# Expert weights read in 4 KB runs, with the second expert's two products run back to back

## The chip, the cores and the metric

The kernel runs on one core of one Trainium2 chip. The metric is the device time of one execution in microseconds, the median of three runs: 222.31 us before the change (221.52 to 224.03). The profile is of one execution, whose span is 219.5 us by the profiler's clock.

## The reference

Two blocks follow each other. The first is a gated recurrence over four sequences of 5056 steps, 256 channels wide. The second takes each of the 20224 results as a token, picks one of eight experts for it by a gate, keeps per expert the 80 tokens with the largest gate probability, and runs a two-layer network on those. All other rows of the output are zero.

```python
for t in range(S):                       # S = 5056, D = 256, four sequences
    h = f[:, t] * h + (1.0 - f[:, t]) * x[:, t]
    y[:, t] = h
...
logits = x @ w_gate                      # x = y.reshape(20224, 256), 8 experts
expert_idx = np.argmax(logits, axis=1)
gate_w = probs[np.arange(N), expert_idx]
out = np.zeros((N, D), dtype=np.float32)
for e in range(E):                       # the best 80 tokens of each expert
    h = np.maximum(x[tok_idx] @ w1[e], 0.0)            # w1[e]: 256 x 1024
    out[tok_idx] = gate_w[tok_idx, None] * (h @ w2[e])  # w2[e]: 1024 x 256
```

Everything is float32. The inputs of the recurrence are 20.7 MB each, the output is as large, and the experts' weights are 16.8 MB (1 MB for each of the two matrices of an expert).

## The kernel before

**The recurrence.** The sequences are cut into 40 units of 512 steps. For each unit the kernel loads gate and input (`load`, L224 and L227), forms the gate on ScalarE, multiplies on GpSimd, turns both to channels on partitions with TensorE (L247), and scans along time on VectorE (L264), into `h_all`, which stays in SBUF. The gate's logits (L276) and the candidates per expert follow in the same loop, one group of four units behind.

**Clearing the output.** The whole output has to be zero before rows are scattered into it. `clear` copies zeros in pieces of up to 1 MB, all issued from the SP queue: from a spare part of `h_all` while the units run (`clear_some`), from rows of the output that are zero already (DRAM to DRAM, the form with no `zero` given, L158), and from a zero tile in SBUF (L163). `clear_blocks(m)` issues m such blocks. With the last unit's load two blocks go out (L437). Nineteen blocks and a rest are cleared by hand-placed calls. The last one, of 0.75 MB, is issued by the first `more` in the experts' stage.

**Selecting.** After the last unit, VectorE, ScalarE and TensorE work out which 80 tokens each expert keeps (L561 to L645), ending in `trow`, the token numbers by expert. TensorE runs dummy products (`busy`, L181) through these waits.

**The experts.** The order of instructions on each engine is the order in which the code names them; nothing is rearranged. For an expert, `gather` copies its 80 columns out of `h_all` one by one, 24 on VectorE, 32 on ScalarE and 24 on GpSimd (L689); `scaled` multiplies them by a per-channel factor (L698); `hidden` is the first product, 32 products into two tiles `h_ps` (L711); `relu` runs on ScalarE (L720); `result` is the second product, eight products into `y_ps` (L727); `finish` scales the rows on VectorE (L733); `scatter` writes them to their places in the output with an indirect DMA from GpSimd (L736), which has to wait for the clears and for the scatter before it. `settle` (L647) works out where the rows go (`slots_down`: `gsl`, `goal`) and whether the selection was certain (`doubts`). The loop at L767 does, for expert e, the gather of e + 2, the first product of e + 1, the second of e, and the scatter of e - 1.

**The weights.** `weights` (L497) loads a matrix as two halves of 0.5 MB into `wring`, a ring of seven buffers. One of these first holds the zero tile. The halves of the first matrix (`which == 1`, L503) are its two halves of columns: a partition gets two runs of 2 KB. The halves of the second (L507) are its two halves of rows: a partition gets four runs of 1 KB. `order` lists the matrices in the order of loading: first and second of expert 0, first of expert 1, and then in turns the first of e + 1 and the second of e. Three matrices are loaded ahead; `more(1)` issues the next one, whose DMA waits until the buffer that it takes is free. A load and the clears stand in one queue, so a load lands behind all that was issued before it.

In `hidden` a weight load takes 64 neighbouring columns of one half:

```python
halves[i][:, o, ds(c * P + j, P // 2)]   # i: half of the columns, o: half of the input channels
```

Of the kernel before, what the change touches and what calls it, by code (L numbers as in the profile page):

```python
# [23 lines left out]
def kernel(  # L24
# [146 lines left out]
    def clear_blocks(m, zero=None):  # L171
        clear_some(len(zeros) % R, zero)
        for k, _ in zeros[:m * R:R]:
            clear(k, None, zero)
        del zeros[:m * R]
# [7 lines left out]
    with tc.tile_pool(name="ld", bufs=4) as ld, \  # L183
# [237 lines left out]
        for n in range(-AHEAD, n_unit):  # L421
            unit(load, n + AHEAD)
            unit(gate, n + 2)

            g, b = divmod(n - 1, B)
            if g > 0 and b == 0:
                aside(g - 1)
            unit(enter, n + 2)
            unit(lambda m: to_channels(m, sts, sps, pss, "sp"), n + 1)
            unit(lambda m: to_channels(m, uts, ups, psu, "up"), n + 1)  # L430
            unit(decay, n + 1)
            unit(scan, n)
            some_of(of_group, 1)
            for jobs in of_batches:
                some_of(jobs, 1)
            unit(logits, n - 1)
            if n + AHEAD == n_unit - 1:  # L437
                clear_blocks(2)
            elif 2 <= n < n_unit - AHEAD:
                clear_some(1, spare(4 if n < 27 else 2 if n < 31 else 1))  # L440
            if n > 0 and n % B == 0:
                g = n // B - 1
                of_group += [[lambda g=g: by_token(g)]]
                if g < ALONE:
                    of_group[-1] += [lambda g=g: shifted(g)]
                    of_group += [[lambda g=g: chosen(g)]]
# [41 lines left out]
                                        imm_value=-2.0)  # L488


    wring = ctx.enter_context(tc.tile_pool(name="wring", bufs=7))
    FH, CH = F // 2, FC // 2
    order = [(1, 0), (2, 0), (1, 1)]
    for e in range(1, E):
        order += ([(1, e + 1)] if e + 1 < E else []) + [(2, e)]

    def weights(which, e):  # L497
        halves = []
        for i in range(2):
            t = wring.tile([P, DC * FH], F32, name="w_sb", tag="w_sb")  # L500
            if which == 1:
                t = t.rearrange("p (o f) -> p o f", o=DC)
                nc.sync.dma_start(out=t, in_=w1[e][:, ds(i * FH, FH)].rearrange(  # L503
                    "(o p) f -> p o f", p=P))
            else:
                t = t.rearrange("p (c d) -> p c d", c=CH)
                nc.sync.dma_start(out=t, in_=w2[e][ds(i * FH, FH)].rearrange(  # L507
                    "(c p) d -> p c d", p=P))
            halves.append(t)
        return halves  # L510

# [3 lines left out]
    zero = wring.tile([P, R * D], F32, name="w_sb", tag="w_sb")  # L515
    nc.sync.dma_start(out=zero.rearrange("p (k d) -> p k d", k=R), in_=out_z[:, 0:R])
    w_sb[order[0]] = weights(*order[0])
    clear_blocks(5, zero)
    for key in order[1:3]:
        w_sb[key] = weights(*key)  # L520
    clear_blocks(3)
# [21 lines left out]
    def slots_down(flat, sp):  # L543

        nc.tensor.transpose(sp, flat, ident[:2 * E, :2 * E])
        nc.vector.tensor_copy(gsl, sp[:, ds(E, E)])
        far = consts.tile([K, E], F32, name="far", tag="far")
        nc.vector.tensor_scalar(out=far, in0=gsl, scalar1=0.0, scalar2=AWAY,
                                op0=ALU.is_le, op1=ALU.mult)
        nc.vector.tensor_tensor(goal, sp[:, :E], far, ALU.add)  # L550
# [96 lines left out]
    def settle():  # L647


        low = consts.tile([P, DEEP], F32, name="low")  # L650
        d = doubts
        slots_down(flat, kept[:K, ds(K, 2 * E)])
        nc.vector.tensor_scalar(out=low, in0=taken, scalar1=-2.0, scalar2=2.0,  # L653
                                op0=ALU.mult, op1=ALU.add)
        nc.vector.tensor_tensor(low, low, vals, ALU.add)
        nc.vector.tensor_reduce(d[:, 4:5], low, AX.X, ALU.min)
        nc.vector.tensor_reduce(d[:, 5:6], tops[:, :, TOP - 1], AX.X, ALU.max)
        nc.vector.tensor_copy(d[:, 0:1], taken[:, DEEP - 1:])
        nc.vector.tensor_tensor(d[:, 1:2], d[:, 5:6], d[:, 4:5], ALU.is_ge)
        nc.vector.scalar_tensor_tensor(out=d[:, 2:3], in0=vals[:, ds(TOP - 1, 1)],  # L660
                                       scalar=vals[:, ds(TOP, 1)], in1=taken[:, ds(TOP, 1)],
                                       op0=ALU.is_le, op1=ALU.mult)
        nc.vector.tensor_scalar(d[:, 3:4], off[:, 2:3], float(capacity), off[:, 1:2],
                                ALU.min, ALU.not_equal)
# [6 lines left out]
    def experts(again):  # L671
        with tc.tile_pool(name="xp", bufs=2) as xp, \
# [8 lines left out]
            def gather(e, between={}):  # L681
                X[e] = xp.tile([P, DC, K], F32, name="xe", tag="xe")
                k = 0
                for engine, copy, n in ways:
                    _, at_tok = nc.values_load_multi_w_load_instructions(
                        trow[ds(e, 1), ds(k, n)], engines=(engine,), min_val=0, max_val=N - 1,
                        skip_runtime_bounds_check_because="token numbers come from iota")
                    for j, v in enumerate(at_tok):
                        copy(X[e][:, :, ds(k + j, 1)], h_all[:, :, ds(v, 1)])  # L689
                        if copy == nc.scalar.copy and j + 1 in between:  # L690
                            between[j + 1]()
                    k += n
# [7 lines left out]
            def hidden(e):  # L700
                HID[e] = mp.tile([P, FC, K], F32, name="hid", tag="hid")
                xt = XT.pop(e)
                halves = w.pop((1, e))
                ps = []
                for i in range(2):
                    h_ps = psh.tile([P, CH, K], F32, name="h_ps", tag="h_ps")

                    for c in range(CH):
                        for o in range(DC):
                            for j in range(0, P, P // 2):  # L710
                                nc.tensor.matmul(h_ps[ds(j, P // 2), c],  # L711
                                                 halves[i][:, o, ds(c * P + j, P // 2)],
                                                 xt[:, o], start=o == 0, stop=o == DC - 1,
                                                 skip_group_check=True)
                    ps.append(h_ps)
                return ps
# [5 lines left out]
            def result(e):  # L722
                y_ps = psy.tile([K, D], F32, name="y_ps", tag="y_ps")
                halves = w.pop((2, e))
                hid = HID.pop(e)
                for c in range(FC):
                    nc.tensor.matmul(y_ps, hid[:, c], halves[c // CH][:, c % CH],  # L727
                                     start=c == 0, stop=c == FC - 1)
                return y_ps
# [10 lines left out]
            def more(m):  # L740
                for key in late[:m]:
                    w[key] = weights(*key)
                del late[:m]
                clear_blocks(len(clears))
# [9 lines left out]
            gather(1, {8: lambda: relu(0, ps, [0]), 24: lambda: relu(0, ps, [1])})  # L754
            scaled(1)
            more(1)
            gather(2)
            y_ps = result(0)
            more(1)
            scaled(2)  # L760
            if not again:
                settle()
            finish(0, y_ps)
            ps = hidden(1)
            relu(1, ps)
            more(1)
            for e in range(1, E):  # L767
                if e + 2 < E:
                    gather(e + 2)
                if e + 1 < E:  # L770
                    ps = hidden(e + 1)
                    relu(e + 1, ps)
                    more(1)
                y_ps = result(e)
                if e == 1 and not again:
                    total = psl.tile([1, 4], F32, name="total", tag="rivals")
                    nc.tensor.matmul(total, ones, doubts[:, :4], start=True, stop=True)
                more(1)
                if e + 2 < E:
                    scaled(e + 2)  # L780
                finish(e, y_ps)
                scatter(e - 1)
                if e == 1 and not again:
                    found = consts.tile([1, 1], F32, name="found")
                    nc.vector.tensor_reduce(found, total, AX.X, ALU.add)
                    nc.vector.tensor_copy(doubt, found)
                if e == E - 2 and not again:
                    unsure.append(nc.values_load(
                        doubt, min_val=0, max_val=4 * P,
                        skip_runtime_bounds_check_because="a sum of 4 * P flags"))  # L790
# [89 lines left out]
```

## Time and profile before

| What | Value |
|---|---|
| Time, median of three runs | 222.31 us (221.52 to 224.03) |
| Span of the profile | 219.5 us |
| TensorE busy | 195.6 us (89%) |
| VectorE busy | 160.8 us (73%) |
| ScalarE busy | 140.3 us (64%) |
| GpSimd busy | 133.1 us (61%) |
| Bytes moved by DMA | 80.62 MB, 367 GB/s over the span |
| Share of the 16 DMA engines taken by the SP queue | 94.9% |
| Of that, expert weights | 32 loads of 512 KB, 7.1 us from issue to landing (median) |

The page gives each engine's busy time, the chain of work that ended last, and groups of instructions by line, engine and tile. In a line of a group or of the timeline, the name of a tile before the arrow is what is written, the names after it are what is read. PE is a product on TensorE, PEld its weight load, DVE is VectorE, ACT ScalarE, POOL GpSimd, SP the queue that issues the loads and clears. A float32 product appears as two records. Times in a timeline are us from the start of the span. The share of DMA can go slightly over 1, as packets overlap.

### The profile page before, as it was taken

What the parts mean: (1) busy time and instruction counts of PE and PEld (TensorE: products, weight loads), DVE (VectorE), ACT (ScalarE), POOL (GpSimd) and SP (SyncE); (2) the same over time, 40 slices, a digit from 0 to 9 for tenths busy, and PEclk for the clock granted to TensorE, in tenths of its full rate; (3) what the DMA queues carried; (4) which work ended last, traced back from release to release, by engine and by line L of the source; (5) the groups of instructions that cost most, each with busy time, mean ns of one, the idle gap of its engine ahead of it and who ended that gap; (6) DMA issues with size and microseconds to landing.
All of it is one profiled execution on the core that took longest, in us unless ns stands there. A gap on an engine that the chain in (4) does not pass through costs nothing.

```text
span 219.5 us, 6776 instructions
## 1 busy us (share of the span) xinstructions
PE 195.6 (89%) x2145; PEld 151.5 (69%) x2145; DVE 160.8 (73%) x437; ACT 140.3 (64%) x440; POOL 133.1 (61%) x271
## 2 busy tenths in 40 slices
PE   7589999999999699999969999788796789999990
PEld 7457777777777477767747776777775667787750
DVE  5687789797979879899786998995556726665110
ACT  3587786877689967787796875151566754665100
POOL 4489578777876689777649881121557365656021
PEclk9999999999999999999999999999999699999996
DMA  6999999999999999999999998999999999999710
GB/s 154 412 418 417 419 418 420 418 415 419 414 419 417 420 414 419 415 417 417 414 401 296 339 367 275 404 416 388 397 382 332 353 393 394 393 385 375 271 37 21
DMA packets 31564, 80.62 MB, mean 367 GB/s; under 512 B 3232, under 2 KB 12832, under 8 KB 30816
## 3 DMA queue, kind: packets, MB, share of 16 engines
q1 hardware_dynamic: 30592, 79.44, 94.9%
q0 software_dynamic: 384, 0.66, 0.9%
q8 instruction: 19, 0.31, 0.5%
q14 instruction: 25, 0.20, 0.2%
q10 hardware_dynamic: 544, 0.01, 0.1%
HBM read 65.28 MB, written 21.36 MB: 395 GB/s over the span
## 4 chain that ended last, share of the span: by engine, by line
PE 43%; DMA 29%; DVE 9%; issue 7%; POOL 4%; ACT 3%; SPq 2%; POOLq 1%; DVEq 0%; ACTq 0%
DMA out_dram<-y,goal 14%; PE lg L276 12%; PE sp L247 12%; PE up L247 12%; DMA out_dram<-out_dram 11%; DMA x_t<-in_x_dram 4%; POOL x_t L240 4%; PE warm L181 2%; DVE h_all L264 2%; PE lt L292 2%; DVE at L596 1%; ACT f_t L232 1%; PE kept L641 1%; DVE beat L615 1%; SPq L227 1%
## 5 line engine op out<-in xcount | busy, mean ns | idle before, releaser
L240 POOL TENSOR_TENSOR x_t<-f_t,x_t 128x1024 f32<-128x1024 f32 (+2 forms) x40 | 93.4, 2338 | 33.9 <-DMA x_t<-in_x_dram 13.7
L264 DVE TENSOR_TENSOR_SCAN h_all<-h_all,up 128x512 f32<-128x512 f32 (+1 forms) x80 | 95.5, 1243 | 4.7 <-ACT h_all L258 2.7
L258 ACT ACTIVATE h_all<-sp,nomlb 128x512 f32<-128x512 f32 (+1 forms) x80 | 50.0, 677 | 7.3 <-PE sp L247 7.3
L232 ACT ACTIVATE f_t<-f_t 128x1024 f32<-128x1024 f32 (+1 forms) x40 | 42.3, 1059 | 15.7 <-DMA f_t<-in_f_logit_dram 15.7
L247 PEld LDWEIGHTS sp<-ident,f_t 128*128 128x128 f32 (+1 forms) x320 | 34.0, 140 | 19.7 <-issue 10.3
L247 PE MATMUL sp<-ident,f_t 128*128 128x128 f32 (+1 forms) x320 | 43.8, 279 | 2.7 <-ACT h_all L258 2.3
L247 PE MATMUL up<-ident,x_t 128*128 128x128 f32 (+1 forms) x320 | 42.0, 273 | 4.6 <-POOL x_t L240 2.2
L276 PE MATMUL lg<-h_all,wg 128*32 128x128 f32 (+1 forms) x640 | 43.1, 400 | 0.0
L247 PEld LDWEIGHTS up<-ident,x_t 128*128 128x128 f32 (+1 forms) x320 | 35.3, 140 | 6.7 <-POOL x_t L240 3.3
L689 ACT COPY xe<-h_all 128x2 f32 x256 | 25.4, 190 | 14.7 <-issue 11.6
L689 POOL COPY xe<-h_all 128x2 f32 x192 | 24.3, 196 | 13.0 <-issue 11.3
L689 DVE COPY xe<-h_all 128x2 f32 x192 | 22.7, 177 | 12.6 <-issue 12.6
L727 PE MATMUL y_ps<-w_sb,hid 128*80 128x256 f32 x128 | 29.3, 383 | 1.8 <-DMA w_sb<-in_moe_w_dram 1.6
L276 PEld LDWEIGHTS lg<-h_all,wg 128*32 128x32 f32 x640 | 18.4, 118 | 11.7 <-issue 4.3
L727 PEld LDWEIGHTS y_ps<-w_sb,hid 128*80 128x80 f32 x128 | 18.5, 150 | 10.3 <-issue 1.8
L711 PE MATMUL h_ps<-xt,w_sb 128*64 128x80 f32 x512 | 21.0, 244 | 3.9 <-DVE low L653 2.5
L711 PEld LDWEIGHTS h_ps<-xt,w_sb 128*64 128x64 f32 x512 | 19.7, 145 | 5.8 <-issue 3.1
L736 POOL DMA_INDIRECT out_dram<-y,goal x8 | 7.5, 939 | 21.1 <-DMA out_dram<-y,goal 11.3
L181 PE MATMUL warm<-ident 128*128 128x128 f32 x140 | 18.3, 291 | 1.4 <-POOL ident masks.py:199 1.4
L181 PEld LDWEIGHTS warm<-ident 128*128 128x128 f32 x140 | 17.6, 206 | 1.5 <-POOL ident masks.py:199 1.4
L733 DVE TENSOR_SCALAR y<-y_ps,gsl 80x256 f32<-80x256 f32 x8 | 3.8, 478 | 14.1 <-PE y_ps L727 14.1
L720 ACT ACTIVATE hid<-h_ps 128x320 f32<-128x320 f32 x16 | 6.7, 431 | 7.6 <-PE h_ps L711 7.4
(116 smaller groups left out, 100.4 us busy)
## 6 DMA issues: line engine op xcount, KB each, us to landing
f_t<-in_f_logit_dram SPq DMA_DIRECT2D x36, 512.0 KB, 7.9
x_t<-in_x_dram SPq DMA_DIRECT2D x36, 512.0 KB, 8.3
w_sb<-in_moe_w_dram SPq DMA_DIRECT2D x32, 512.0 KB, 7.1
out_dram<-h_all SPq DMA_DIRECT2D x34, 256.0 KB, 8.1
out_dram<-out_dram SPq DMA_DIRECT2D x5, 1024.0 KB, 11.1
out_dram<-w_sb SPq DMA_DIRECT2D x5, 1024.0 KB, 9.7
f_t<-in_f_logit_dram SPq DMA_DIRECT2D x4, 448.0 KB, 6.8
x_t<-in_x_dram SPq DMA_DIRECT2D x4, 448.0 KB, 7.2
```

Source lines behind the costliest of these rows:

```text
L181: nc.tensor.matmul(warm, ident, ident, start=True, stop=True)
L232: nc.scalar.activation(s_t, s_t, ACT.Sigmoid, scale=-1.0)
L240: nc.gpsimd.tensor_tensor(u_t[:, cut:], sts[n][:, cut:], u_t[:, cut:], ALU.mult)
L247: nc.tensor.transpose(ps[:, r:R * k:R], src[n][:, r, ds(o * P, P)], ident[:k, :k])
L258: nc.scalar.activation(columns(n, o), sps.pop((n, o)), ACT.Identity, scale=nomlb[:, ds(o, 1)], bias=1.0)
L264: nc.vector.tensor_tensor_scan(h, h, ups.pop((n, o)), h_all[:, o, ds(spot(n) - 1, 1)] if n >= B else 0.0, ALU.mult, ALU.add)
L276: nc.tensor.matmul(lgs[g][ds(r * LC, LC), b, :k], wg[:, o], columns(n, o)[:, r::R], start=o == 0, stop=o == DC - 1, skip_group_check=True)
L689: copy(X[e][:, :, ds(k + j, 1)], h_all[:, :, ds(v, 1)])
L711: nc.tensor.matmul(h_ps[ds(j, P // 2), c], halves[i][:, o, ds(c * P + j, P // 2)], xt[:, o], start=o == 0, stop=o == DC - 1, skip_group_ch ...
L720: nc.scalar.activation(HID[e][:, ds(i * CH, CH)], ps[i], ACT.Relu)
L727: nc.tensor.matmul(y_ps, hid[:, c], halves[c // CH][:, c % CH], start=c == 0, stop=c == FC - 1)
L736: nc.gpsimd.indirect_dma_start(out=out, out_offset=bass.IndirectOffsetOnAxis(ap=goal[:, ds(e, 1)], axis=0), in_=Y.pop(e), in_offset=None, ...
```

## The change

The change gives every partition one run of 4 KB in each half of the weights. For the first matrix a half is now half of its rows (input channels) with all 1024 columns; for the second, partition p takes the four neighbouring rows 4p to 4p + 3 of a half. The inner channels then have to be counted alike on both sides: channel 4k + c of a half is column k of the c-th product, so a weight load of `hidden` takes 64 columns with a step of four elements, and both halves are needed for each output.

With it goes a new order. The second matrix of expert 1 is loaded ahead of the first of expert 2, and the second product of expert 1 precedes the first of expert 2. `slots_down` is taken out of `settle` and stands before the first product of expert 1, `settle` moves behind the second `finish`, the ReLU of expert 1 moves into ScalarE's gather of expert 2 (after 12 and 24 copies), and the loop starts at expert 2. One block of clears moves from the zero tile (five blocks to four) to the place of the last unit's load (two to three). The aim is longer runs for the DMA engines, fewer waits of TensorE for weights, and work for the DMA queue before the zero tile arrives.

```diff
             if n + AHEAD == n_unit - 1:
-                clear_blocks(2)
+                clear_blocks(3)
...
-    order = [(1, 0), (2, 0), (1, 1)]
-    for e in range(1, E):
+    order = [(1, 0), (2, 0), (1, 1), (2, 1), (1, 2)]
+    for e in range(2, E):
...
             if which == 1:
-                t = t.rearrange("p (o f) -> p o f", o=DC)
-                nc.sync.dma_start(out=t, in_=w1[e][:, ds(i * FH, FH)].rearrange(
-                    "(o p) f -> p o f", p=P))
+                nc.sync.dma_start(out=t, in_=w1[e][ds(i * P, P)])
+                t = t.rearrange("p (i k c) -> p i c k", i=2, c=CH)
             else:
                 t = t.rearrange("p (c d) -> p c d", c=CH)
                 nc.sync.dma_start(out=t, in_=w2[e][ds(i * FH, FH)].rearrange(
-                    "(c p) d -> p c d", p=P))
+                    "(p c) d -> p c d", c=CH))
...
-    clear_blocks(5, zero)
+    clear_blocks(4, zero)
...
-        slots_down(flat, kept[:K, ds(K, 2 * E)])
...
-                                                 halves[i][:, o, ds(c * P + j, P // 2)],
+                                                 halves[o][:, i, c, ds(j, P // 2)],
...
             more(1)
-            gather(2)
             y_ps = result(0)
+            if not again:
+                slots_down(flat, kept[:K, ds(K, 2 * E)])
+            ps2 = hidden(1)
+            gather(2, {12: lambda: relu(1, ps2, [0]), 24: lambda: relu(1, ps2, [1])})
             more(1)
             scaled(2)
+            finish(0, y_ps)
+            y_ps = result(1)
+            more(1)
+            gather(3)
+            ps = hidden(2)
+            relu(2, ps)
+            more(1)
+            scaled(3)
+            finish(1, y_ps)
+            scatter(0)
             if not again:
                 settle()
-            finish(0, y_ps)
-            ps = hidden(1)
-            relu(1, ps)
-            more(1)
-            for e in range(1, E):
+            for e in range(2, E):
```

## The prediction

> **What bounds the kernel now.** I read the page's chain first (the work that ended last), then the stretches table, the timeline of TensorE, the same chain in order of time, and the groups of weight loads.
>
> The page's chain, by engine:
>
> ```profile
> PE 43%; DMA 29%; DVE 9%; issue 7%; POOL 4%; ACT 3%; SPq 2%; POOLq 1%; DVEq 0%; ACTq 0%
> ```
>
> Up to 122 us the chain is TensorE's recurrence work, which the change does not touch; from 134 to 159 us it is VectorE's selection, also untouched. What can move is the stage after 159 us, the experts. TensorE there (h_ps is an expert's first product, y_ps its second; start, length, what the idle time waited for):
>
> ```profile
> 159.46 2.44 PE L711 MATMUL h_ps<-xt,w_sb 128*64 128x80 f32 x64 [1.41 <-issue]
> 162.09 3.78 PE L727 MATMUL y_ps<-w_sb,hid 128*80 128x256 f32 x16 [0.20 <-ACT hid L720]
> ...
> 165.94 2.44 PE L711 MATMUL h_ps<-xt,w_sb 128*64 128x80 f32 x64
> 170.91 3.92 PE L711 MATMUL h_ps<-xt,w_sb 128*64 128x80 f32 x64 [2.54 <-DVE low L653]
> 176.46 3.65 PE L727 MATMUL y_ps<-w_sb,hid 128*80 128x256 f32 x16 [1.62 <-DMA w_sb<-in_moe_w_dram]
> ...
> 180.16 2.43 PE L711 MATMUL h_ps<-xt,w_sb 128*64 128x80 f32 x64
> 182.53 3.68 PE L727 MATMUL y_ps<-w_sb,hid 128*80 128x256 f32 x16
> ```
>
> Call these h0, y0, h1, h2, y1, h3, y2 by expert. From 176.46 us on TensorE has no gap until y7 ends at 213.56: one expert each 5.97 us. Before that lie three losses: 2.5 us idle ahead of h2, 1.5 us in h2 itself (3.92 for 2.43), 1.6 us ahead of y1, which waits for its weights. The DMA queue is why. Stretches (PE, PEld, DVE, ACT and POOL busy, granted clock, DMA share, GB/s):
>
> ```profile
> 134.00:138.00 4.00, 3.29 (x55) 2.06 (x54) 3.55 (x8) 2.63 (x5) 0.00 (x0) 1.00 0.80 227
> 142.00:151.00 9.00, 7.16 (x59) 6.65 (x57) 8.10 (x32) 4.10 (x16) 2.26 (x9) 1.00 1.03 419
> 154.00:155.80 1.80, 1.80 (x19) 1.80 (x18) 0.31 (x3) 0.00 (x0) 0.15 (x2) 1.00 1.08 378
> 162.50:166.00 3.50, 3.50 (x19) 2.06 (x18) 1.67 (x14) 2.11 (x20) 2.04 (x17) 1.00 1.01 321
> 177.00:189.00 12.00, 12.00 (x164) 9.20 (x163) 5.07 (x36) 7.84 (x68) 8.04 (x50) 1.00 1.07 395
> ```
>
> The queue is full (share about 1) except in 134 to 138, and its speed follows the runs: 419 GB/s for the clears in 4 KB pieces (142 to 151), 378 for the second matrix in 1 KB pieces (154 to 155.8), 408 for the first in 2 KB pieces (a stretch at 139), 321 for the clears from DRAM to DRAM (162.5 to 166). In 177 to 189 both TensorE and the queue are full; TensorE wins narrowly, since the slack between a half's landing and its use, read from the landings, grows from 1 us at y2 to 2.5 us at y7. The chain by time shows a second path as long:
>
> ```profile
> 161.23 13.83 DMA out_dram<-out_dram
> ...
> 177.32 5.37 DMA out_dram<-y,goal
> ...
> 211.22 2.30 DMA out_dram<-y,goal
> ...
> 214.35 0.91 POOL out_dram L736
> ```
>
> The last clear, issued at 161.23, lands at 175.06; only then may the first scatter go, and every scatter waits for the one before (5.1 to 5.6 us each while the queue is full, plus 0.8). It ends level with TensorE. So a gain needs both: weights of experts 1 and 2, and the last clear, landing earlier.
>
> **What the Trainium skill says.** *DMA: Bandwidth & Descriptors*, "Why small descriptors are slow (HBM only)": every packet carries a fixed overhead, so short ones run below the engine's rate; the trace agrees (378 against 419 GB/s). *SBUF — State Buffer*, "Door 1: The DMA port swizzle": memory lines are 16 bytes, and an access that crosses to a new line each time pays a penalty. The new weight read steps four fp32, exactly 16 bytes, so every element is on a new line. *TensorE: Matmul & The Clock Gate*, "LDWEIGHTS": a load costs its columns over 1.2 GHz, an estimated 53 ns for 64. The trace agrees: 137 ns for 64 columns, 192 for 128 in a stream, 0.86 ns a column. Same page, "The HAM clock gate": after a mostly idle window of 3.4 us the clock is halved; the trace has one such stretch, 171.6 to 175.0, after the idle time before h2.
>
> **The change part by part.**
>
> *4 KB runs.* A half of 0.524 MB at 378, 408 and 419 GB/s takes 1.39, 1.29 and 1.25 us: 0.14 us saved per half of the second matrix, 0.04 of the first. Up to and with the weights of experts 0 and 1 and the first of expert 2 that is 4 × 0.14 + 6 × 0.04 = 0.8 us. Later, 0.36 us an expert, hidden: TensorE is the bound there. It does shorten the backlog behind which each scatter lands.
>
> *One clear earlier.* A third block clear goes out ahead of the zero tile's load, which waits for buffers until 134.3 us; one clear from the zero tile goes. The bytes stay the same, but the thin stretch 134 to 138 gets work: 4 us × (419 − 227)/419 = 1.8 us of queue at most. The zero tile's load itself is slow there and the four clears after it still wait for its landing, so I take 0.4 to 1.2, and 0.5 with the first part's overlap: the last weights needed for h2 (second half of expert 2) land where y1's second half lands now, 177.64, less 0.8 and 0.5, so about 176.4.
>
> *Order.* Expert 1's second matrix comes ahead of expert 2's first. It takes over the latter's landings, 170.78 and 172.08, less 1.0 to 1.2: about 169.7 and 170.9. h1 ends at 168.4, so y1 runs 169.8 to 173.5 (its second half needs its weights 1.8 us after the start, 171.6). The ReLU that y1 needs now stands inside ScalarE's gather, after 12 and 24 of 32 copies; that gather starts at 166.25 with 98 ns a copy, so the ReLUs come at 167.5 and 169.1, behind no wait that binds. What queues behind them on ScalarE is the rest of the gather, 0.9 us later, for an h2 that waits until 176.4 anyway. Then h2 stands from 176.5 to 178.9. Before, the same four products (h1, h2, y1 after y0) were done at 180.11: 1.2 us gained. The swap alone gives nothing: both weights were needed before h3, and one of the two stages always waits for the last half. The idle time only moves, to 2.9 us between y1 and h2.
>
> *Settling later, slots earlier.* Eleven small VectorE operations of 0.15 to 0.2 us move behind the second finish. The 2.54 us that h2 waited for them vanish, but the weights bind in their place: nothing. The three for the slots go ahead of a gather that has 5 us to spare.
>
> *Halves by input rows.* h needs both halves at its start (one was enough) and frees both at its end: 1.2 us earlier, 1.2 later. With slack of 1 to 2.5 us and a queue that now gains 0.36 us an expert on TensorE, nothing from h3 on; for h2 it is in the 176.4.
>
> *The step of 16 bytes.* The disputed cost: no weight load of h_ps kind has a step in this trace. The nearest rows:
>
> ```profile
> L247 PEld LDWEIGHTS sp<-ident,f_t 128*128 128x128 f32 (+1 forms) x320 | 34.0, 140 | 19.7 <-issue 10.3 <-ACT h_all L258 4.6 <-ACT f_t L232 3.9
> L711 PEld LDWEIGHTS h_ps<-xt,w_sb 128*64 128x64 f32 x512 | 19.7, 145 | 5.8 <-issue 3.1 <-DVE far L548 2.7
> L292 PEld LDWEIGHTS lt<-ident,ls 128*128 128x128 f32 (+1 forms) x40 | 5.5, 207 | 1.6 <-ACT ls L283 1.1
> ```
>
> L247 and L292 are both loads for transposes of 128 columns; L292 reads with the same step of four, and takes 67 ns more, 0.5 ns a column. In a stream, though, its transposes follow each other at 119 ns instead of 109, 0.93 ns a column. h_ps has 32 pairs of loads in 2.43 us, 76 ns a pair. Low end: 0.93 ns a column is a ceiling on the read; 64 columns take 60 ns, still under 76: nothing. Middle: 0.5 ns a column on top of 0.86: 87 ns, 0.4 us a stage. High end: the rate halves as it did for the transposes: 110 ns, 3.7 us a stage. I take nothing, because a plain load already reads at 0.86 ns a column, where the stepped read stands at 0.93.
>
> Sum: 222.3 − 1.2 (TensorE's path; the scatters start about 1.2 us earlier too, at 176.1, and catch up as the backlog shrinks) = 221.1, and 0.1 back for a chance of the cold clock: 221.2.
>
> **Rivals.**
> 1. *More of the queue's loss comes back.* For: 227 GB/s in 134 to 138 is an open 1.8 us, and the DRAM clears run at 423 GB/s at 159 to 161.5 but 321 later. All 1.8 and 0.8 recovered puts h2's weights at 175.0 and its end at 177.5, 2.6 us gained; the freed queue and the scatters' spacing (0.2 us over TensorE's) bring some 0.5: 219.2. Against: the zero tile's load is a chain of its own.
> 2. *The stepped read doubles the weight load.* TensorE is the bound from h2 on, with six h stages left: 6 × 1.25 = 7.5 us, less 1.2: 228.6. h0 and h1 would hide in the wait for weights. For: 207 against 140 ns, and the skill's 16-byte line. Against: the stream's 0.93. With the middle cost 6 × 0.4 − 1.2 = +1.2: 223.5.
> 3. *The idle 2.9 us before h2 halves the clock* for a 3.4 us window (as after 2.54 us before) and the last weights are no earlier: h2 takes 3.9, up to 180.4, and no gain remains, 222.5, or 225 with h4 late as well, whose second half can only be issued when h2 has freed its buffer.
>
> **How the numbers follow.** Forecast 221.2: 0.36, with rival 3's mild form in it (within 1%, 220.1 to 224.5). Rival 1, 219.2: 0.33 (faster by over 1%). Rival 2, 228.6: 0.26, and rival 3's 225: 0.05 (slower, 0.31). The range leaves out the best twentieth and the upper half of rival 2: 218.8 to 228.5.
>
> **What would show it.** Right: weights at about 418 GB/s in a stretch after 177; no thin stretch at 134 to 138; y1 starting at about 169.8, h2 at 176.5 with a wait for its weights; first scatter at 176; h_ps loads of 140 to 150 ns and stages of 2.4 us. Wrong: h_ps stages of 2.8 us or more (rival 2); a wait before h2 under 1 us (rival 1); clock 0.5 after 176 (rival 3). A y1 that waits for its ReLU and not for weights would break the order's step.

## The result, and the profile after

The changed kernel takes 230.89 us (230.38 to 231.33, four runs) where the kernel before, on the same chip, took 223.17 (221.52 to 224.72; the three runs given above and a fourth): a ratio of 1.0346, 95% interval 1.0258 to 1.0435. It is slower by 7.7 us. The forecast was 221.2 us; the nearest case was the second rival, at 228.6.

The page's chain, by engine, of the kernel after:

```profile
PE 63%; DMA 15%; issue 6%; DVE 6%; POOL 4%; ACT 3%; SPq 1%; POOLq 0%; DVEq 0%; ACTq 0%
```

TensorE carries 63% of the chain where it had 43%, and the DMA half of what it had. The clears, and all scatters but the last ones, which together were a second path as long, have left it. The timeline of TensorE says why (start, length, what the idle time waited for; L712 is the first product, L728 the second):

```profile
160.42 4.43 PE L712 MATMUL h_ps<-xt,w_sb 128*64 128x80 f32 x64 [2.27 <-issue]
164.77 3.80 PE L728 MATMUL y_ps<-w_sb,hid 128*80 128x256 f32 x16
...
168.64 4.07 PE L712 MATMUL h_ps<-xt,w_sb 128*64 128x80 f32 x64
172.64 3.68 PE L728 MATMUL y_ps<-w_sb,hid 128*80 128x256 f32 x16
176.76 0.47 PE L712 MATMUL h_ps<-xt,w_sb 128*64 128x80 f32 x4 [0.44 <-DMA w_sb<-in_moe_w_dram]
177.97 7.67 PE L712 MATMUL h_ps<-xt,w_sb 128*64 128x80 f32 x124 [0.74 <-DMA w_sb<-in_moe_w_dram]
185.57 3.68 PE L728 MATMUL y_ps<-w_sb,hid 128*80 128x256 f32 x16
...
189.30 4.07 PE L712 MATMUL h_ps<-xt,w_sb 128*64 128x80 f32 x64
```

From h1 on every first product takes 4.07 us in place of 2.43 (h0 takes 4.43, most of it at a granted clock of 0.50, in 161.64 to 165.05 us); the second product is unchanged at 3.68. The new order did what it was to do: y1 follows h1 without a wait, and in place of the losses ahead of h2 and y1 (2.54 and 1.62 us) stand 0.44 and 0.74 us in h2. But from h2 on nothing hides TensorE, and six stages at 1.64 us more are 9.8 us. The last second product ends at 223.26 us, not 213.56. Where the 1.64 us are, the group of weight loads says (count | busy us, mean ns of one):

```profile
L712 PEld LDWEIGHTS h_ps<-xt,w_sb 128*64 128x64 f32 x512 | 31.7, 217 | 5.3 <-issue 4.4 <-PE y_ps L728 0.8
```

The same load of 64 columns took 145 ns in the mean before (137 at full clock). The stretches show what this does to the queue, and what became of the thin stretch:

```profile
134.00:138.00 4.00, 3.29 (x55) 2.06 (x54) 3.48 (x8) 2.73 (x5) 0.00 (x0) 1.00 1.01 344
138.00:142.00 4.00, 3.19 (x29) 2.95 (x28) 3.60 (x16) 0.65 (x2) 0.98 (x3) 1.00 0.98 346
...
177.00:189.00 12.00, 11.26 (x144) 9.94 (x142) 6.95 (x54) 6.72 (x58) 7.77 (x48) 1.00 0.97 376
189.00:201.00 12.00, 12.00 (x149) 10.33 (x148) 6.70 (x50) 7.56 (x67) 6.90 (x43) 1.00 0.81 284
```

Two of these stretches in the kernel before:

```profile
138.00:142.00 4.00, 3.19 (x29) 2.95 (x29) 3.60 (x15) 0.65 (x2) 0.98 (x3) 1.00 1.04 410
...
189.00:201.00 12.00, 12.00 (x162) 9.23 (x161) 7.86 (x59) 7.95 (x69) 7.90 (x50) 1.00 1.07 386
```

In 134 to 138 us the queue is now full (share 1.01 for 0.80), but at 344 GB/s, and 138 to 142 has dropped to 346, from 410 before. From 189 us on the share is 0.81, where it was 1.07: the queue waits for TensorE to free buffers. TensorE alone is the bound there.

### The profile page after: what moved, and what is told of

Its sections match the earlier page's. It is cut to its first block, busy times and chain, and to the rows that moved or that the text cites. A ratio compares the mean times of both kernels' runs of the same rounds, so it can differ in the third digit from the quotient of the medians.

```text
span 229.4 us, 6777 instructions
## 1 busy us (share of the span) xinstructions
PE 207.7 (91%) x2145; PEld 163.8 (71%) x2145; DVE 160.7 (70%) x437; ACT 141.0 (61%) x440; POOL 133.4 (58%) x271
## 4 chain that ended last, share of the span: by engine, by line
PE 63%; DMA 15%; issue 6%; DVE 6%; POOL 4%; ACT 3%; SPq 1%; POOLq 0%; DVEq 0%; ACTq 0%
PE lg L276 13%; PE sp L247 13%; PE up L247 13%; PE h_ps L712 11%; DMA w_sb<-in_moe_w_dram 8%; PE y_ps L728 7%; DMA x_t<-in_x_dram 4%; POOL x_t L240 3%; DMA out_dram<-y,goal 3%; PE warm L181 2%; PE lt L292 2%; DVE h_all L264 2%; DVE at L598 1%; ACT f_t L232 1%; PE kept L643 1%
## 5 line engine op out<-in xcount | busy, mean ns | idle before, releaser
L712 PE MATMUL h_ps<-xt,w_sb 128*64 128x80 f32 x512 | 32.9, 290 | 3.5 <-issue 2.3
L712 PEld LDWEIGHTS h_ps<-xt,w_sb 128*64 128x64 f32 x512 | 31.7, 217 | 5.3 <-issue 4.4
L728 PE MATMUL y_ps<-w_sb,hid 128*80 128x256 f32 x128 | 29.3, 383 | 0.0
L728 PEld LDWEIGHTS y_ps<-w_sb,hid 128*80 128x80 f32 x128 | 18.7, 151 | 8.2 <-ACT xe L690 0.2
```

The lines of the kernel that those rows point to most:

```text
L712: nc.tensor.matmul(h_ps[ds(j, P // 2), c], halves[o][:, i, c, ds(j, P // 2)], xt[:, o], start=o == 0, stop=o == DC - 1, skip_group_check=True)
```

## The experiments

The theory: the step of 16 bytes alone makes the loss. The rival: order, clears and late weights make it. The first four kernels tell them apart.

**The order without the layout.** The new order and clears, with the layout and the contiguous weight loads of before.

```diff
-                nc.sync.dma_start(out=t, in_=w1[e][ds(i * P, P)])
-                t = t.rearrange("p (i k c) -> p i c k", i=2, c=CH)
+                t = t.rearrange("p (o f) -> p o f", o=DC)
+                nc.sync.dma_start(out=t, in_=w1[e][:, ds(i * FH, FH)].rearrange(
+                    "(o p) f -> p o f", p=P))
...
-                                                 halves[o][:, i, c, ds(j, P // 2)],
+                                                 halves[i][:, o, ds(c * P + j, P // 2)],
```

> The new order, ReLU places and clears with the old layout of the weights (2 KB and 1 KB runs, no step). Theory A: 222 to 224.5. Rival B: 227 or more.

Measured: ratio 1.0038 (1.0000 to 1.0076).

**The layout without the order.** The kernel before with the 4 KB runs and the step of four, its order and clears kept (the edit above the other way round, in the kernel before).

> The old order and clears with the new layout (4 KB runs and the step of four). Theory A: stages of 4.07 us, 230 or more. Rival B: 222 to 224.

Measured: ratio 1.0315 (1.0206 to 1.0424), first products of 4.07 us. The layout makes nearly the whole loss.

**The changed kernel without the step.** Its loads, order and clears kept, but each weight load takes 64 neighbouring columns.

```diff
-                t = t.rearrange("p (i k c) -> p i c k", i=2, c=CH)
+                t = t.rearrange("p (i c k) -> p i c k", i=2, c=CH)
```

> The changed kernel with its loads, order and clears, but each weight load of the first product reads 64 neighbouring columns instead of 64 with a step of four (so hidden channels meet the wrong rows of the second matrix: the output is not the reference's). Theory A (the step sets the time): weight loads back to about 137 ns, a first-product stage back from 4.07 to about 2.45 us, the second expert's end no longer behind; time 222 to 224, level with the kernel before. Rival B (order, clears or late weights set the time): stages of 2.45 us but longer waits in their place, time 227 or more.

Measured: ratio 1.0070 (1.0038 to 1.0102). The weight loads of this kernel:

```profile
L712 PEld LDWEIGHTS h_ps<-xt,w_sb 128*64 128x64 f32 x512 | 18.4, 137 | 4.5 <-issue 3.9 <-DVE low L654 0.5
```

**A step of 8 bytes.** The second matrix in runs of 2 KB, two neighbouring rows per partition, so that the weight load steps by two elements.

```diff
-                t = t.rearrange("p (i k c) -> p i c k", i=2, c=CH)
+                t = t.rearrange("p (i g k s) -> p i g s k", i=2, g=2, s=2)
...
-                    "(p c) d -> p c d", c=CH))
+                    "(g p s) d -> p g (s d)", p=P, s=2))
...
-                                                 halves[o][:, i, c, ds(j, P // 2)],
+                                                 halves[o][:, i, c // 2, c % 2, ds(j, P // 2)],
```

> The changed kernel with a step of two: the second matrix in runs of 2 KB (two neighbouring rows a partition), the first still in runs of 4 KB. Theory A in the form of 16-byte lines (two elements of a line are enough): weight loads at about 137 ns, stages at 2.45 us, 222 to 224. Theory A in the form that any step costs the same: 217 ns, 4.07 us, 231. In between (each element pays by its distance): about 180 ns, 3.2 us, 227.

Measured: ratio 1.0031 (1.0004 to 1.0058). Its weight loads, and TensorE around the reordered products:

```profile
L713 PEld LDWEIGHTS h_ps<-xt,w_sb 128*64 128x64 f32 x512 | 18.5, 138 | 3.6 <-issue 2.4 <-PE y_ps L729 0.5 <-DVE xe L691 0.4
```

```profile
165.90 2.44 PE L713 MATMUL h_ps<-xt,w_sb 128*64 128x80 f32 x64
170.28 5.34 PE L729 MATMUL y_ps<-w_sb,hid 128*80 128x256 f32 x16 [1.94 <-DMA w_sb<-in_moe_w_dram]
...
180.89 3.68 PE L729 MATMUL y_ps<-w_sb,hid 128*80 128x256 f32 x16
```

A step of two costs 1 ns on a load, and the loss of the change is gone but for 0.3%. The rival is out as the cause of the 3.5%. In its place stands a second question: the kernel now has all that the change was to bring, without the cost, and its time still shows no gain (the three kernels above without the step of four stay 0.3 to 0.7% behind the kernel before). y1 waits 1.94 us for its weights and then takes 5.34 us for 3.68, at a granted clock of 0.58 in 170.3 to 173.7.

**A step of 32 bytes.** Weight loads at a step of eight.

```diff
-                t = t.rearrange("p (i k c) -> p i c k", i=2, c=CH)
+                t = t.rearrange("p (i k s) -> p i s k", i=2, s=2 * CH)
```

> The changed kernel with weight loads of 64 columns at a step of eight elements, 32 bytes, in place of four (inner channels meet other rows of the second matrix, so the output is not the reference's). If a load is paid by memory lines of 16 bytes, each touched for one element, nothing changes against the step of four: about 217 ns a load, 4.07 us a first product, 230 to 231 us. If the cost grows with the distance: 290 ns or more, over 5.5 us a first product, over 238 us. If 16 bytes is a special case of a conflict between banks: back to 137 ns and 2.44 us, 224 to 225 us.

```profile
L712 PEld LDWEIGHTS h_ps<-xt,w_sb 128*64 128x64 f32 x512 | 31.8, 218 | 4.4 <-issue 3.3 <-PE y_ps L728 1.0
```

Measured: ratio 1.0336 (1.0239 to 1.0432), and 218 ns, the same as at a step of four. Steps of 4, 8, 16 and 32 bytes give 137, 138, 217 and 218 ns: the cost does not grow with the distance, neither from 4 to 8 bytes nor from 16 to 32. That fits a price for every element that is alone in its line of 16 bytes. The Trainium skill says just this (*SBUF — State Buffer*, "Specifications (TRN2)": a line of 16 bytes needs at least two hits for full bandwidth), and the four numbers agree. A step of 12 bytes was not tried.

**Where the gain went.** Six kernels take the rest apart. First the kernel before with the step of two alone:

> The kernel before with its own order and clears; of the change only the layout, in a form with a step of 8 bytes: the first matrix in runs of 4 KB, the second in runs of 2 KB, weight loads of 64 columns with a step of two. Theory A (only the step of 16 bytes costs): loads 137 to 138 ns, first product 2.44 us; the longer runs save 10 x 0.04 to 4 x 0.14 us of queue up to the last weights that TensorE waits for, so 0.5 to 0.8 us off the wait before y1: 222.5 to 223.4 beside a kernel before at 223.9, ratio 0.995 to 1.0. Rival B (longer runs are themselves no help or a harm, as the new order's kernels with them stand at 1.003): ratio 1.003 or more, with the first product still at 2.44 us.

Measured: 1.0069 (1.0040 to 1.0098), with first products at 2.44 us. The longer runs bring no gain in time, and the expectation of one failed. Then the moved clear alone, and taken out of the step-of-two kernel:

```diff
             if n + AHEAD == n_unit - 1:
-                clear_blocks(2)
+                clear_blocks(3)
...
-    clear_blocks(5, zero)
+    clear_blocks(4, zero)
```

> The kernel before with the moved clear alone: three blocks with the last unit's load, four from the zero tile. The prediction's step for it was a gain of 0.4 to 1.2 us: ratio 0.995 to 0.998. If the clear from DRAM to DRAM only fills the thin stretch at a lower rate and pushes the zero tile's load back: zero tile lands at about 142 us and the time is the same or up to 1 us longer, ratio 1.0 to 1.004.

> The changed kernel with the step of two (runs of 4 and 2 KB), and its clears as in the kernel before: two blocks with the last unit's load, five from the zero tile. If the moved clear is what took the order's gain (it ran from DRAM to DRAM at about 345 GB/s and let the zero tile land 4 us later): zero tile lands at about 138.6 us, y1's weights 0.5 to 1.5 us earlier than with the moved clear, 0.4 to 1.2 us faster than that kernel, ratio to before 0.995 to 1.0. If the moved clear is neutral: ratio 1.003 again, y1 waiting for weights 2 to 3 us and then running at half clock.

Measured: 1.0043 (1.0013 to 1.0073) for the moved clear alone, in the kernel before; 1.0011 (0.9981 to 1.0040) for the step of two without it. Alone, the moved clear costs a little and gains nothing; in the kernel with the step of two (1.0031 with it, 1.0011 without) the difference lies inside the intervals. In the chain in order of time of the kernel with the moved clear alone, the last clear now ends at 162.29 + 14.43 = 176.72 us, where it ended at 175.06, and the scatters start as much later:

```profile
162.29 14.43 DMA out_dram<-out_dram
...
179.13 5.38 DMA out_dram<-y,goal
...
217.15 0.91 POOL out_dram L736
```

Its zero tile landed at 142.8 us in place of 138.6, behind three blocks that go from DRAM to DRAM.

The half clock in y1. The kernel with the step of two and the old clears has it too:

```profile
172.30 5.34 PE L729 MATMUL y_ps<-w_sb,hid 128*80 128x256 f32 x16 [3.60 <-DMA w_sb<-in_moe_w_dram]
```

The same kernel with dummy products ahead of y1:

```diff
+            if not again:
+                busy(psl, 20, "rivals")
             y_ps = result(1)
```

> The changed kernel with the step of two and its clears as before, and 20 dummy products (about 2.2 us) ahead of the second product of expert 1, so that TensorE does not stand idle through its wait for weights. The kernel without them has y1 from 172.30 for 5.34 us at half clock and h2 behind it without a wait, though h2's weights had landed at 177.82. If the cold clock takes part of the order's gain: y1 3.7 us, h2 waiting until 177.8, end 0.8 to 1.4 us earlier, ratio to before 0.993 to 0.998. If the weights bind whatever the clock: no difference, ratio 1.001.

```profile
168.51 4.73 PE L181 MATMUL warm<-ident 128*128 128x128 f32 x40
173.08 3.62 PE L729 MATMUL y_ps<-w_sb,hid 128*80 128x256 f32 x16
176.63 0.36 PE L713 MATMUL h_ps<-xt,w_sb 128*64 128x80 f32 x4
177.31 4.83 PE L713 MATMUL h_ps<-xt,w_sb 128*64 128x80 f32 x124 [0.31 <-DMA w_sb<-in_moe_w_dram]
```

Measured: 1.0056 (1.0029 to 1.0084). y1 keeps its clock (3.62 us), and h2 then waits for its weights, which land at 177.17: no earlier end. The 20 dummies took 4.73 us, twice my estimate, and y1 began 1.6 us after its first half of weights had landed, but it still ended before h2's were there. With these clears the half clock took nothing that was to be had: without the dummies y1 ends at 177.64, and h2's weights land at 177.82. Why the time is 0.4% above that of the kernel without the dummies is open.

Last, six of the eight scatters left out, in the old order and in the new one with the step of two:

```diff
             def scatter(e):
+                if e < E - 2:
+                    Y.pop(e)
+                    return
```

> The kernel before without the scatters of experts 0 to 5 (their rows stay zero in the output); those of 6 and 7 stay. In the profile of before the chain of scatters ends level with TensorE (last scatter issued 0.8 us after the last product), so if the chain of scatters is no bound of its own here: ratio 0.998 to 1.0. If it binds in most executions: 1 us or more faster, ratio 0.995 or less.

> The changed kernel with the step of two in place of four, also without the scatters of experts 0 to 5. With all scatters it stands at 1.003, and its last scatter was issued 3.3 us after the last product ended. If the chain of scatters takes a gain that TensorE has: TensorE's end decides now, 1.2 us (0.5%) or more faster than the old order without the same scatters. If the weights bind and the order gains nothing on TensorE: equal to it within 0.3%.

Measured: 0.9903 (0.9861 to 0.9944) for the old order, 0.9948 (0.9923 to 0.9972) for the new. Without the chain of scatters the old order ends 1% earlier: over its executions that chain, which starts at the last clear, costs the kernel before about that much. (Leaving out six scatters also takes 0.5 MB off the queue, but from 177 us on, where TensorE has no wait for weights.) And with the chain gone the new order is still no faster than the old. So over the executions the order brings TensorE no gain.

A single profile can look otherwise. The last products and the last scatter of the kernel before, and then of the kernel with the step of two and the moved clear:

```profile
206.43 7.13 PE L727 MATMUL y_ps<-w_sb,hid 128*80 128x256 f32 x32
...
214.35 0.91 POOL out_dram L736
```

```profile
205.25 7.13 PE L729 MATMUL y_ps<-w_sb,hid 128*80 128x256 f32 x32
...
215.72 0.91 POOL out_dram L738
```

In this one execution, the fastest of its 20, y1 starts at 170.28 us (forecast: 169.8) and TensorE ends 1.2 us earlier than before, which is the gain that was forecast. But the first scatter goes out at 177.19, not at 176.1, and the last one 1.4 us later than before, so none of it reaches the end. With the old clears TensorE ends at 213.90, later than the 213.56 of the kernel before. So two limits stand: the last weights, whose landing differs between executions, leave TensorE 1.2 us in the best of these profiles, and the scatters take that.

**A version that beats both?** The runs pointed to faster clears. Five kernels tried it; none is faster than the kernel before. First the zero tile set by GpSimd, which the stretches show idle in 134 to 138 us:

```diff
-    nc.sync.dma_start(out=zero.rearrange("p (k d) -> p k d", k=R), in_=out_z[:, 0:R])
+    nc.gpsimd.memset(zero, 0.0)
```

> The kernel before; the zero tile is set by GpSimd (128x1024 takes 0.94 us in the profile of before, and GpSimd is idle from 134 to 138 us) in place of a load from the output that is issued at 134.3 and lands at 138.6. If the thin stretch 134 to 138 us is what a better placed clear could win back, as the prediction's step and its first rival had it (up to 1.8 us): first clear issued at about 135.5, y1's weights 1.5 us or more earlier, ratio 0.992 to 0.995. If nothing of it reaches the end: ratio 1.0.

Measured: 1.0110 (1.0047 to 1.0173). GpSimd's timeline in this kernel:

```profile
138.85 0.20 POOL L312 MEMSET shift<- 128x128 f32 x1 [5.58 <-DVE sm L340]
139.85 0.78 POOL L354 TENSOR_TENSOR gm<-oh,sm 128x128 f32<-128x128 bf16 x2 [0.80 <-DVE sm L347]
140.56 0.95 POOL L516 MEMSET w_sb<- 128x1024 f32 x1
```

I had named the idle time and not what stands ahead in the engine's order: two instructions that wait for VectorE. The tile was zero at 141.5, not at 135.5, and the first clear went out 2.9 us later than before. Then, with that fill kept, the last four clears from a second, lasting zero tile of 2 KB a partition, without DRAM to DRAM, in both orders:

```diff
-    clear_blocks(3)
+    clear_blocks(3, zero_s)
...
-                clear_blocks(len(clears))
+                clear_blocks(len(clears), zero_s)
```

> The kernel before with the zero tile set by GpSimd and the last four clears (three blocks and the rest) from a second, lasting zero tile of 2 KB a partition in place of DRAM to DRAM. Those run at 1 MB in 3.3 us in 160 to 170 us, the clears from SBUF at 2.45 us: about 0.8 us each, 2.5 to 3 us in all ahead of the weights of expert 2 and the last clear, and 1.5 us from the earlier zero tile. If the last weights bind, h2 and y1 no longer wait, TensorE is the bound from h1 on and 3 to 4 us are gained: ratio 0.982 to 0.988. If the chain of scatters or TensorE takes over early: 0.992.

> The new order with the step of two, the clears' places as before, and the two zero tiles of the kernel above. Same queue gains of about 4 us; y1's weights land at about 168.3, when h1 ends, so the new order has no wait left: ratio 0.980 to 0.988, within 0.3% of the old order with the same zero tiles if both orders end up bound by TensorE; 0.5% or more faster than it if the order brings a gain of its own.

Measured: 1.0196 (1.0139 to 1.0253) and 1.0246 (1.0171 to 1.0321). And with the first zero tile loaded as before, and the second set after the selection:

> The kernel before with the last four clears from a lasting zero tile of 2 KB a partition, set by GpSimd after the selection, when it is idle, in place of DRAM to DRAM. 3.3 us a block against about 2.6: 2.5 us less queue ahead of the last clear and of y1's weights, so the first scatter at about 175 us. If the clears bind scatters and weights: 1.5 to 2.5 us faster, ratio 0.989 to 0.993. If the register loads ahead of the gathers stall as in the kernels with two zero tiles (6.2 us ahead of the second gather there): slower, 1.01 or more.

> The changed kernel with the step of two and the same clears from the lasting zero tile. If the clears were what held back the new order: y1 waits for weights less than 1 us and keeps the full clock, ratio 0.985 to 0.992, and faster than the old order with the same clears. If stalls of the register loads come with it: slower, 1.01 or more.

Measured: 1.0101 (1.0044 to 1.0158) and 1.0104 (1.0028 to 1.0181; the second rests on two executions). The clears did get faster (the last one landed at 173.96 us in the old order, for 175.06), but the copies of the gathers stalled, and the first scatter went out at 180.03 us, 2.7 later than before. Waits in 157 to 172 us (us in total, times, longest), of the kernel before and then of the old order with the second tile; "issue" ahead of `xe` is where the token numbers are loaded into registers:

```profile
ACT xe L689 <- issue: 3.7, 3, 1.8
DVE xe L689 <- issue: 3.1, 3, 1.4
...
POOL xe L689 <- issue: 2.5, 2, 1.3
```

```profile
POOL xe L690 <- issue: 10.4, 2, 7.2
ACT xe L690 <- issue: 10.0, 3, 3.9
DVE xe L690 <- issue: 7.7, 4, 3.1
```

What holds the copies up here is not settled.

## Why the prediction was wrong

**The step of 16 bytes: the step that failed.** "Low end: 0.93 ns a column is a ceiling on the read; 64 columns take 60 ns, still under 76: nothing." The 0.93 was right; the comparison was not. The 76 ns are those of a pair: a float32 product appears as two records and has two weight loads, which the group's count shows (x512 for eight experts of 32 products). The transposes at L292 are one record each (40 of them). So a pair reads 2 × 64 columns, 2 × 60 = 120 ns, and not 60. Loads within one stage, before and after (count, shortest/median/longest in ns, first and last start in us):

```profile
L711 PEld LDWEIGHTS h_ps<-xt,w_sb x33: 136/137/137, 186.2 to 187.3; 128*64 128x64 f32 x33
```

```profile
L712 PEld LDWEIGHTS h_ps<-xt,w_sb x21: 193/217/218, 189.3 to 190.5; 128*64 128x64 f32 x21
```

Before, 32 intervals fill 1.1 us, after, 20 fill 1.2 us: about 34 and 60 ns a load. Taken from the single records, the pairs of successive products start 69 ns apart before and 120 after. That is 0.94 ns a column, the transposes' rate. The row that I took as evidence for nothing gave the cost almost exactly: 31 intervals × (120 − 69) ns = 1.58 us a stage of the 1.64 measured. A plain load of this kind reads at 69 / 128 = 0.54 ns a column, so the 0.86 that I set against it, from the difference of two durations (192 ns for 128 columns, 137 for 64), was no rate either. Nor is there the agreement that the prediction saw in it with the Trainium skill (*TensorE: Matmul & The Clock Gate*, "LDWEIGHTS": columns over 1.2 GHz, an estimated 53 ns for 64): two such loads start within 69 ns here, and the measurement decides. The argument from lines of 16 bytes pointed the right way and lost to the wrong division.

**The second rival** had the cause, and its size was low: 110 ns a pair and 1.25 us a stage, from "the rate halves", for 120 ns and 1.64 us. (Its 110 for 76 ns a pair would be 32 × 34 ns = 1.1 us a stage, so the 1.25 doesn't follow from it.) That h0 and h1 would hide in the wait for weights held: in the two profiles the last product ends 9.7 us later (223.26 for 213.56), which is about h2 to h7 at 1.64 us each. The median times differ by 7.7, because the profile of before is of an execution of 221.43 us, where the median is 223.17.

**The clear one earlier**, forecast as a gain of 0.5 us: ratio 1.0043 alone, a loss of about 1 us. The thin stretch was filled, as forecast, but at 344 GB/s, with copies from DRAM to DRAM, and the zero tile landed 4.2 us later, so the fast clears (419 GB/s) began later.

**The runs**, forecast at 0.8 us up to h2's weights: not seen in the time (1.0069 in the old order). In the trace of the kernel with the step of two and the old clears, the stretch from the zero tile's landing to the last of those weights is 177.82 − 139.63 = 38.2 us, for 177.64 − 138.60 = 39.0 before (38.3 with the dummies, 38.5 in the old order with longer runs): 0.5 to 0.9 us are in the queue. But the zero tile's landing differs by over 1 us between executions, and single profiles do not resolve the rest. The sign of about 418 GB/s after 177 us was not seen: in 178 to 190 us the old order moves 409 with the longer runs and 396 without, in 190 to 202 us 383 and 381. The 419 behind it was of clears, which go the other way, from SBUF to DRAM. Why the old order with longer runs is 0.7% slower is open.

**The order**: "the swap alone gives nothing", and "the idle time only moves", both held (1.0038 with the old layout, the moved clear in it). The half clock that I had put into h2's wait (third rival) came in y1; with the old clears it costs nothing that the weights don't cost anyway. The ReLU inside the gather was free, as forecast: y1 waits for weights and for nothing else. The later settling was nearly so: in the kernel without the step a wait of 0.39 us in h2 is put down to it.

**The second path** "ends level with TensorE": in the one profile, yes; over the runs the chain of scatters binds, by 1%. My sum moved TensorE's end and the scatters' start together, to 176.1 us; the scatters start from the last clear, which did not come earlier, and they started at 178.36 in the changed kernel and at 177.19 with the step of two. So this step failed too: it would have cost the forecast its 1.2 us even without the step of 16 bytes.

## What to carry to other kernels

Before a read rate is compared with a spacing, count what one spacing holds: a float32 product here has two loads. Let no weight load step over float32 so far that each element is alone in its 16 bytes; a step of two keeps long runs (2 KB for one matrix here) without that cost, though they gained no time here. Idle time on an engine helps only if nothing that waits stands ahead of the new instruction in its order.

## What the runs showed of the hardware

- A weight load of 64 float32 columns at a step of 1, 2, 4 and 8 elements: 137, 138, 217 and 218 ns; a first product of 32 such products: 2.43, 2.44, 4.07 and about 4.1 us.
- Transposes of 128 float32 columns, with one load each, follow each other at 109 ns with a step of 1 and at 119 ns with a step of 4: there the same step costs 10 ns.
- A wait of 1.94 us on TensorE was followed by a stretch near half clock (0.58 in 3.4 us), in which a second product took 5.34 us instead of 3.68.
- In the kernel with the zero tile set by GpSimd, a VectorE operation that takes 0.17 us (L345) took 0.57 beside that fill; in the kernel with two fills it took 1.02.
